# Five pairs of rounds instead of four convolved by VectorE, in a short convolution fused with a multiplicative feed-forward

## The chip, the cores and the metric

One core of a Trainium2 chip. The metric is the device time of one execution in microseconds (us); a time given for a kernel is the median of several runs. The engines are TensorE (PE in the profile; its weight loads are PEld), VectorE (DVE), ScalarE (ACT), GpSimd (POOL) and SyncE (SP). Each runs its own instructions in order; they wait for each other through semaphores. SP issues most DMAs (queue SPq) and computes nothing; GpSimd issues the DMAs that convert float32 to bfloat16 on the way (queue POOLq).

## The reference

`x` is 8 sequences of 3904 tokens with 192 channels. Each of 8 heads (24 channels each) has 7 taps, normalised by a softmax; every channel is convolved along its sequence, causally, with its head's taps. The result, 31232 x 192, goes through a feed-forward with a product in the middle:

```
w = exp(weight - max); w = w / (sum(w) + 1e-09)        # (8, 7)
out[b, s, h*24+g] = sum_k w[h, k] * x_padded[b, s + k, h*24+g]
a = x @ w1 ; b = x @ w2                                # 192 -> 1024
h = (a * b) @ w3 ;  return h @ w_out                   # 1024 -> 1024 -> 192
```

Weights are float32 at the interface; the kernel computes in bfloat16 with float32 accumulation.

## The kernel before

`w3` and `w_out` are multiplied once at the start into `W_sb` (1024 x 192), so that each token needs two products: the first, `x @ w1` and `x @ w2` with the product of both, and the second, that times `W_sb`.

The tokens are seen as two streams of TS = 15616 tokens (`NS` = 2, four sequences each) that go side by side: one on partitions 0 to 63, one on 64 to 127. A round R is 512 tokens of each stream; there are 31 rounds, the last of 256. The channels stand in three groups of 64 (`NP` = 3). `first_product(R)` (L471) makes for each of 8 blocks of 128 features `pa` and `pb` in PSUM (6 matmuls of 64 x 512 each), ScalarE copies `pa` to `asb` (L493), VectorE multiplies it with `pb` into `abT` (L495). `second_product(R, r)` (L505) makes 32 matmuls into `ops`, ScalarE copies them to `osb` (L516), SP sends that out (L521). PSUM has four slots of two banks, which `pa`, `pb`, `ops` and the convolution's `cps` take in turn; `osb` has five buffers.

The instructions are emitted in an order written out by hand: a start with rounds 0 to 2, in which weights are loaded and swapped between partition halves and `W_sb` is made (`w3_turn`, `w3_product`), and then phases (L672). Phase 0 has no first products; phase p from 1 to 14 has the first products of rounds 2p + 1 and 2p + 2. After them each phase has the second products of rounds 2p and 2p + 1 (the last phase: all that are left), so these run two rounds or more behind.

The convolved operand of the first products is made in one of two ways.

By TensorE: the tokens are cut into windows of 32 that give 26 results each, gathered in batches (`SIZES`, windows per stream). `x_jobs` has GpSimd's DMA queue load a batch as bfloat16 into `xb`; `conv` (L300) multiplies it by the banded matrix `Aband` (32 x 32 pieces) into `cps`, and ScalarE (`A`) or VectorE (`V`) evicts that to `convo`; `store` (L334) writes it to DRAM (`rows`), and `transposes(R)` (L390) has SP read it back transposed into a ring of four rounds, `xT`. Batches 0 to 3 belong to the start. From batch 4 on a batch is convolved in units of 2 or 4 heads (L646), put between second products by `places` (L649). A unit of 4 heads is 64 matmuls, of 2 heads 32, which hold twice the windows each. In the phases that have a task (below) both evictions are ScalarE's, otherwise one is VectorE's (L662).

By VectorE, for the rounds of the phases in `SIDE` (4, 7, 10 and 13): one task is one channel group of one such phase, 1024 tokens of both streams. `side_cast` has GpSimd's queue copy `x` as bfloat16 to DRAM (`rows_c`, L417), one issue a stream; `side_transpose` has SP read it transposed into `raw` (L427, two issues); `side_conv` (L430) multiplies by the second-last tap into the float32 sum `acc` (L437), adds five products (L444) and writes the seventh tap's sum to `side`. Where a sequence begins inside the task, the five sums are made in two pieces. The taps come from `wC`, which SP loads (L403) and GpSimd copies to the second partition half (L674). A task runs in one of the three phases ahead of its own, so phases 1 to 12 have one task each. `side_conv` is emitted ahead of the second products. `operand` (L454) reads `side` or `xT`.

GpSimd's DMA jobs of a phase (`jobs`, L653) are spread over its first products: at `points`, GpSimd copies a corner of `abT` (`pace`, L679) and then issues a share. In the start, `later_loads` (L614) issues the loads of batch 3, of `w_out` and `w3`, then batch 4, the first task's two casts, and batch 5.

Of the kernel before, what the change touches and what calls it, by code (L numbers as in the profile page):

```python
# [8 lines left out]
FP32 = mybir.dt.float32  # L9
BF16 = mybir.dt.bfloat16  # L10
AX = mybir.AxisListType
ALU = mybir.AluOpType
ACT = mybir.ActivationFunctionType
# [3 lines left out]
def kernel(  # L17
# [10 lines left out]
    nc = tc.nc  # L28

    B, S, D = x.shape  # L30
    H, K = weight.shape
    G = D // H
# [4 lines left out]
    NS = 2  # L37
    TS = B * S // NS
    CH = 512
    NR = -(-TS // CH)  # L40
    RING = 4 * CH
    LAG = 2
    Q = 64
    NP = D // Q
    C = 32
    ST = C - PAD
    LAG_ROWS = (LAG + 1) * CH
    SIDE = (4, 7, 10, 13)
    SIZES = [20, 20, 20, 40, 40, 40, 80, 80, 80, 32]
    NB = len(SIZES)  # L50
    FIRST = [sum(SIZES[:b]) for b in range(NB)]
    XN = 20 * D
# [2 lines left out]
    def phase_of(R):  # L55
        return (R - 1) // 2
# [10 lines left out]
    conv_rounds = [R for R in range(NR) if phase_of(R) not in SIDE]  # L67
    ring_of = {R: i for i, R in enumerate(conv_rounds)}
    t0 = (LAG + 3) * CH
    spans = [(0, t0), (t0, t0 + SIZES[4] * ST), (t0 + SIZES[4] * ST, (2 * SIDE[0] + 1) * CH)]  # L70
    for q, nxt in zip(SIDE, SIDE[1:] + (NR,)):
        spans.append(((2 * q + 3) * CH, min((2 * nxt + 1) * CH, TS)))
    wins = []
    for i, (t0, t1) in enumerate(spans):
        ws = windows(t0, t1)
        size = sum(SIZES[:4]) if i == 0 else SIZES[3 + i]
# [85 lines left out]
    def load_x(b):  # L162
        for part in range(len(parts_of(b))):
            for f in x_jobs(b, part):
                f()
# [107 lines left out]
    p = group(1, 0).start  # L273
# [130 lines left out]
                              in_=taps_d[h:h + 1, :].to_broadcast([c1 - c, K]))  # L404
            c = c1

    raw_of, side_of = {}, {}

    def side_span(p):
        return (2 * p + 1) * CH, (2 * p + 3) * CH  # L410

    def side_cast(p, k):
        t0, t1 = side_span(p)

        def job(r):
            def run():
                nc.gpsimd.dma_start(  # L417
                    out=rows_c[t0 - HALO:t1, k, r * Q:r * Q + Q],
                    in_=x_rows[r * TS + t0 - HALO:r * TS + t1, k * Q:k * Q + Q])
            return run  # L420
        return [job(r) for r in range(NS)]

    def side_transpose(p, k):
        t0, t1 = side_span(p)
        raw_of[p, k] = stage.tile([128, HALO + 2 * CH], BF16, tag="w3T", bufs=2, name="raw")
        for lo, hi in ((t0 - HALO, t0 + CH), (t0 + CH, t1)):
            nc.sync.dma_start_transpose(  # L427
                out=raw_of[p, k][:, HALO + lo - t0:HALO + hi - t0], in_=rows_c[lo:hi, k, :])

    def side_conv(p, k):  # L430
        t0, t1 = side_span(p)
        if p not in side_of:
            side_of[p] = stage.tile([128, NP, 2 * CH], BF16, tag="w3b0", bufs=1, name="side")
        raw = raw_of.pop((p, k))
        acc = stage.tile([128, 2 * CH], FP32, tag="w3b4", bufs=1, name="acc")
        starts = [z for z in range(0, TS, S) if t0 <= z < t1]
        nc.vector.tensor_scalar(  # L437
            out=acc, in0=raw[:, HALO - 1:HALO - 1 + t1 - t0], scalar1=wC[:, k, K - 2:K - 1],
            scalar2=None, op0=ALU.mult)
        for z in starts:  # L440
            nc.vector.memset(acc[:, z - t0:z - t0 + 1], 0.0)

        def add(out, lo, hi, d):
            nc.vector.scalar_tensor_tensor(  # L444
                out=out, in0=raw[:, HALO + lo - t0 - d:HALO + hi - t0 - d],
                scalar=wC[:, k, K - 1 - d:K - d], in1=acc[:, lo - t0:hi - t0],
                op0=ALU.mult, op1=ALU.add)

        for d in range(2, K):
            for lo, hi in zip([t0] + [z + d for z in starts], starts + [t1]):  # L450
                add(acc[:, lo - t0:hi - t0], lo, hi, d)
        add(side_of[p][:, k, :], t0, t1, 0)

    def operand(R, k, rs):  # L454
        if phase_of(R) in SIDE:
            t0 = R * CH - side_span(phase_of(R))[0]
            return side_of[phase_of(R)][rs, k, t0:t0 + width(R)]
        a = ring_of[R] * CH % RING
        return xT[k][rs, a:a + width(R)]
# [45 lines left out]
    def second_product(R, r):  # L505
        ab = abT_of[R]
        ng = width(R) // 128
        ops = banks("ops")
        for g in range(ng):
            for jt in range(JT):  # L510
                nc.tensor.matmul(  # L511
                    ops[:, g // 2, (g % 2) * D:(g % 2) * D + D],
                    ab[:, jt, r, g * 128:(g + 1) * 128], W_sb[:, jt, :],
                    start=(jt == 0), stop=(jt == JT - 1))
        osb = slot([128, ng, D], FP32, "osb")
        nc.scalar.copy(out=osb.rearrange("p (a g) d -> p a (g d)", g=2),  # L516
                       in_=ops[:, 0:ng // 2, 0:2 * D])
        n = ng if R < NR - 2 else ng // 2
        for g in range(0, ng, n):
            t0 = r * TS + R * CH + g * 128  # L520
            (nc.scalar if g and (R, r) == (NR - 1, NS - 2) else nc.sync).dma_start(  # L521
                out=out[t0:t0 + n * 128, :].rearrange("(g p) d -> p g d", p=128),
                in_=osb[:, g:g + n, :])
        if r == 1:
            del abT_of[R]
# [79 lines left out]
        swap_w(k, HC + 256, DFF, P)  # L605
    load_w3(0, 4, range(2, 4))

    def seq(*fs):
        def run():
            for f, *a in fs:  # L610
                f(*a)
        return run

    def later_loads():  # L614
        nc.gpsimd.tensor_scalar(out=taps, in0=taps, scalar1=total, scalar2=None, op0=ALU.mult)
        load_x(3)
        load_wo()
        load_w3(4, 2)
        load_w3(6, 2)
        load_x(4)  # L620
        for f in side_cast(SIDE[0], 0):
            f()
        load_x(5)

    first_product(0, {
        0: seq((swap_w, 1, 256, HC, A, (1,))),
# [11 lines left out]
               (conv, 3, 0, 96, (A,), (0,)), (conv, 3, 0, 96, (V,), (1,))),  # L638
        4: seq((w3_product, 4), (w3_product, 6),
               (conv, 3, 96, 96, (A,), (0,)), (conv, 3, 96, 96, (V,), (1,)),  # L640
               (store, 3), (transposes, 3), (transposes, 4))})


    phases = [()] + [(R, R + 1) for R in range(LAG + 1, NR, 2)]
    assert phases[-1][-1] == NR - 1
    units = [(b, h, n) for b in range(4, NB)  # L646
             for n in [max(v for v in (2, 4) if v * shape_of(b)[1] * G <= CH)]
             for h in range(0, H, n)]
    places = {0: (0, 1), 1: (0, 2), 2: (2,), 3: (0, 1, 2), 5: (0, 2), 6: (0, 2),  # L649
              8: (0, 2), 9: (0, 2), 10: (0,), 11: (0,)}  # L650
    assert sum(map(len, places.values())) == len(units)
    tasks = {q - NP + k: (q, k) for q in SIDE for k in range(NP)}
    jobs = {p: side_cast(*tasks[p + 1]) for p in range(1, len(phases)) if p + 1 in tasks}  # L653
    for p, b, part in ((1, 6, 0), (2, 6, 1), (3, 7, 0), (4, 7, 1), (6, 8, 0), (7, 8, 1), (9, 9, 0)):
        jobs[p] = jobs.get(p, []) + x_jobs(b, part)
    points = ((0, 1), (0, 3), (0, 5), (0, 7), (1, 2), (1, 4))
    sent = [LAG + 3]
    due = []

    def convolve(p):  # L660
        b, h, n = units.pop(0)
        conv(b, h * G, n * G, (V, A) if p not in tasks else (A, A))  # L662
        if h + n == H:
            store(b)
            while sent[0] < len(conv_rounds) and \
                    min((conv_rounds[sent[0]] + 1) * CH, TS) <= spans[b - 3][1]:
                due.append(conv_rounds[sent[0]])
                sent[0] += 1
# [1 line left out]
    pace = const.tile([1, 2], BF16)  # L670
    done = 0
    for p, rounds in enumerate(phases):  # L672
        if p == 0:
            P(out=wC[Q:128], in_=wC[0:Q])  # L674
        todo = jobs.pop(p, [])

        def issue(R, ft, n):
            def run():
                P(out=pace, in_=abT_of[R][0:1, ft, 1, 0:2])  # L679
                for _ in range(min(n, len(todo))):  # L680
                    todo.pop(0)()
            return run

        each = -(-len(todo) // len(points))
        for j, R in enumerate(rounds):
            first_product(R, {ft: issue(R, ft, each) for a, ft in points if a == j and todo})
        assert not todo
        for b in {u[0] for u in units[:3]}:
            for xb, p0, w in zero_rows.pop(b, []):
                nc.gpsimd.memset(xb[p0:p0 + PAD, w, :], 0.0)  # L690
        if p + 1 in tasks:
            side_transpose(*tasks[p + 1])
        if p in tasks:
            side_conv(*tasks[p])
        last = NR if p == len(phases) - 1 else done + 2
        seconds = [(R, r) for R in range(done, last) for r in range(NS)]
        done = last
        for n, (R, r) in enumerate(seconds):
            (last_product if (R, r) == (NR - 1, NS - 1) else second_product)(R, r)
            if n in places.get(p, ()):  # L700
                convolve(p)
        for R in due[:2]:
            transposes(R)
        del due[:2]
# [31 lines left out]
```

## Time and profile before

| what | us |
|---|---|
| median of 3 runs | 516.99 (516.53 to 517.62) |
| profiled execution, its own time | 516.74 |
| its span | 514.9 |
| second products of phase 0 begin | 52.25 |
| first products of phase 1 begin | 64.44 |
| first products of phase 14 begin | 482.47 |
| last matmuls begin | 510.17 |

The span is what lies between the first and the last instruction; 1.84 us of the run lie around it. The profile's groups give the busy time of all instructions of one line and shape, their mean in ns, and after the bar the idle time of that engine just before them with what ended it. In the chain of waits, time is put down to the work that the end waited for. A row of the stretch view has the busy time of each engine between two times, a bracket behind each with the instructions. A matmul's end is modelled, so a busy TensorE is not by itself a TensorE at its peak. The granted TensorE clock of the profiled execution is 0.999.

### The profile page before, as it was taken

How to read it: one execution, taken by the hardware profiler on the slowest of the kernel's cores; microseconds unless marked ns; L12 is line 12 of the kernel's file. 1: busy time of each engine (PE TensorE's matmuls, PEld its weight loads, DVE VectorE, ACT ScalarE, POOL GpSimd, SP SyncE). 2: the span in 40 equal slices, each digit the busy share in tenths (PEclk: the TensorE clock that was granted, in tenths of full speed). 3: DMA queues.
4: the chain of work that ended last, by engine and by line, in shares of the span. 5: the costliest groups of instructions: out<-in, count | busy, mean ns of one | idle time of the engine just before them, and what ended most of it. 6: DMA issues, size and time to landing. Idle time of an engine off the chain costs nothing.

```text
span 514.9 us, 14364 instructions
## 1 busy us (share of the span) xinstructions
PE 510.1 (99%) x6148; PEld 334.5 (65%) x6148; DVE 418.2 (81%) x410; ACT 340.2 (66%) x392; POOL 90.3 (18%) x191
## 2 busy tenths in 40 slices
PE   9999999999999999999999999999999999999997
PEld 4446946758567585675856758567585675846787
DVE  7898389699796997979979899797997979977370
ACT  7786476674768737677576475767747657376562
POOL 9965021040220401002030010320101000000000
PEclk9999999999999999999999999999999999999999
DMA  9999599898575998039599872835949171210304
GB/s 141 150 166 185 123 163 203 166 146 153 71 96 138 184 153 160 23 124 82 105 150 179 187 72 80 106 45 144 155 115 144 23 190 27 75 51 1 123 1 155
DMA packets 149744, 61.19 MB, mean 119 GB/s; under 512 B 102708, under 2 KB 149680, under 8 KB 149680
## 3 DMA queue, kind: packets, MB, share of 16 engines
q1 hardware_dynamic: 88848, 42.73, 37.3%
q0 software_dynamic: 60672, 17.44, 35.0%
q8 instruction: 48, 0.79, 0.6%
q14 instruction: 16, 0.13, 0.1%
q10 hardware_dynamic: 160, 0.10, 0.1%
HBM read 35.16 MB, written 34.85 MB: 136 GB/s over the span
## 4 chain that ended last, share of the span: by engine, by line
PE 95%; POOL 3%; ACT 0%; issue 0%; DVE 0%; POOLq 0%
PE ops L511 32%; PE pa L486 30%; PE pb L486 30%; PE cps L318 2%; POOL ws L214 1%; PE wps L579 1%; POOL xb L152 1%; PE tps L365 0%; PE ops L532 0%; DVE abT L495 0%; POOL w3b L560 0%; POOL wn L220 0%; POOL wn L221 0%; POOL wn L223 0%; POOL wn L222 0%
## 5 line engine op out<-in xcount | busy, mean ns | idle before, releaser
L495 DVE TENSOR_TENSOR abT<-asb,pb 128x1024 bf16<-128x1024 bf16 x240 | 292.9, 1221 | 71.6 <-ACT asb L493 56.0
L493 ACT CAST asb<-pa 128x1024 bf16<-128x1024 f32 x244 | 247.0, 1012 | 63.3 <-PE pa L486 63.1
L486 PEld LDWEIGHTS <-wn 64*128 64x128 bf16 x1488 | 138.2, 94 | 85.1 <-issue 2.2
L486 PEld LDWEIGHTS <-ws 64*128 64x128 bf16 x1488 | 131.1, 94 | 71.3 <-POOL ws L214 1.1
L511 PE MATMUL ops<-W_sb,abT 128*128 128x192 bf16 x1936 | 165.5, 247 | 0.0
L511 PEld LDWEIGHTS <-abT 128*128 128x128 bf16 x1936 | 158.1, 98 | 8.5 <-issue 8.1
L486 PE MATMUL pb<-xT,wn 64*128 64x512 bf16 (+1 forms) x552 | 146.7, 372 | 0.0
L486 PE MATMUL pa<-xT,wn 64*128 64x512 bf16 (+1 forms) x552 | 145.8, 372 | 0.2
L486 PE MATMUL pa<-xT,ws 64*128 64x512 bf16 (+1 forms) x552 | 145.9, 372 | 0.0
L486 PE MATMUL pb<-xT,ws 64*128 64x512 bf16 (+1 forms) x552 | 144.7, 372 | 0.1
L516 ACT COPY osb<-ops 128x768 f32<-128x768 f32 (+1 forms) x61 | 48.4, 793 | 99.0 <-PE ops L511 99.0
L444 DVE SCALAR_TENSOR_TENSOR acc<-raw,wC,acc 128x1024 f32<-128x1024 bf16 (+10 forms) x90 | 78.7, 925 | 1.3
L679 POOL COPY pace<-abT 1x2 bf16<-1x2 bf16 x52 | 9.1, 174 | 282.7 <-DVE abT L495 282.7
L486 PE MATMUL pb<-side,wn 64*128 64x512 bf16 x192 | 52.0, 376 | 0.0
L486 PE MATMUL pa<-side,wn 64*128 64x512 bf16 x192 | 51.8, 376 | 0.0
L486 PE MATMUL pa<-side,ws 64*128 64x512 bf16 x192 | 51.8, 377 | 0.0
L486 PE MATMUL pb<-side,ws 64*128 64x512 bf16 x192 | 51.4, 376 | 0.0
L152 POOL DMA_DIRECT2D xb<-in_x_dram x64 | 40.8, 642 | 13.0 <-issue 6.3
L327 ACT CAST convo<-cps 128x640 bf16<-128x640 f32 (+4 forms) x70 | 39.1, 637 | 1.6 <-PE cps L318 1.5
L417 POOL DMA_DIRECT2D rows_c<-in_x_dram x24 | 18.6, 778 | 6.9 <-issue 6.9
L444 DVE SCALAR_TENSOR_TENSOR side<-raw,wC,acc 128x1024 bf16<-128x1024 bf16 x12 | 15.4, 1285 | 0.4
L318 PE MATMUL cps<-xb,Aband 32*32 32x120 bf16 (+2 forms) x1088 | 13.3, 233 | 0.0
(65 smaller groups left out, 101.4 us busy)
## 6 DMA issues: line engine op xcount, KB each, us to landing
out_dram<-osb SPq DMA_DIRECT2D x58, 384.0 KB
xb<-in_x_dram POOLq DMA_DIRECT2D x28, 240.0 KB, 6.4
rows_c<-in_x_dram POOLq DMA_DIRECT2D x24, 130.0 KB, 4.8
rows<-convo SPq DMA_DIRECT2D x9, 240.0 KB
xb<-in_x_dram POOLq DMA_DIRECT2D x8, 228.0 KB, 10.4
rows<-convo SPq DMA_DIRECT2D x9, 150.0 KB
xb<-in_x_dram POOLq DMA_DIRECT2D x8, 168.0 KB, 4.4
rows<-convo SPq DMA_DIRECT2D x9, 120.0 KB
```

Of the source, the lines that this page charges most:

```text
L152: nc.gpsimd.dma_start(out=tiles[js[0]][0][group(r, e), s:s + w, :], in_=bass.AP(tensor=x.tensor, offset=(r * TS + t - PAD) * D, ap=[[D, C] ...
L214: f(out=wsw[k][Q * h:Q * h + Q, lo:hi], in_=wn[k][Q - Q * h:2 * Q - Q * h, lo:hi])
L318: nc.tensor.matmul(o.rearrange("p (w g) -> p w g", g=wd)[:, :, c - c0:c1 - c0], Aband[group(r, e), h, :], xb[group(r, e), s:s + m, c:c1], ...
L327: f(out=convo[:, e::E, k, :, lo:lo + c] .rearrange("p w r g -> p r w g"), in_=src[:, :, :, o:o + c])
L417: nc.gpsimd.dma_start(out=rows_c[t0 - HALO:t1, k, r * Q:r * Q + Q], in_=x_rows[r * TS + t0 - HALO:r * TS + t1, k * Q:k * Q + Q])
L444: nc.vector.scalar_tensor_tensor(out=out, in0=raw[:, HALO + lo - t0 - d:HALO + hi - t0 - d], scalar=wC[:, k, K - 1 - d:K - d], in1=acc[:, ...
L486: nc.tensor.matmul(p[:, r, f * N:f * N + N], w_of(i, k, r)[rs, ft * 128:(ft + 1) * 128], operand(R, k, rs), start=(k == 0), stop=(k == NP ...
L493: nc.scalar.copy(out=asb[:, :, 0:per * N], in_=pa[:, :, 0:per * N])
L495: nc.vector.tensor_tensor(out=ab[:, f0, :, 0:N], in0=asb[:, :, 0:N], in1=pb[:, :, 0:N], op=ALU.mult)
L511: nc.tensor.matmul(ops[:, g // 2, (g % 2) * D:(g % 2) * D + D], ab[:, jt, r, g * 128:(g + 1) * 128], W_sb[:, jt, :], start=(jt == 0), stop ...
L516: nc.scalar.copy(out=osb.rearrange("p (a g) d -> p a (g d)", g=2), in_=ops[:, 0:ng // 2, 0:2 * D])
L679: P(out=pace, in_=abT_of[R][0:1, ft, 1, 0:2])
```

## The change

`SIDE` becomes (3, 6, 9, 12, 14): five phases, the last with 768 tokens a stream instead of 1024 (rounds 29 and 30). The batches become 20, 20, 20, 40, 40, 80, 80, 80, 40: one batch less than before, 420 windows instead of 452, in 16 units from batch 4 on instead of 18. `spans` is worked out in a loop and begins a new batch after each `SIDE` phase.

The fifteen tasks (five phases by three groups) are laid out one after the other over the phases from 0 on, by a room of 6.8 sums a phase where a sum of 1024 tokens counts 1 and of 768 counts 0.75. This gives one task each in phases 0 to 11, in phase 12 one and a half of the shorter tasks and in phase 13 the other one and a half. A task's first product, by the second-last tap, is made by ScalarE (`side_first`), and VectorE makes six sums (`side_sums`). `side_steps`, called ahead of each second product, emits them: the first product at its place n, the sums as soon as their task's first product has been emitted. For the tasks of phases 0 to 12 that begin a phase, n is 0.

There are now two `acc`, five `raw` and two `side` buffers, taken once in `side_tiles`, in space that `w3b` and `w3T` had in the start, and one `side` of its own. Task 0's casts are issued in `later_loads` ahead of batch 4, and task 1's behind it, followed by the first half of batch 5; the other casts go to the phases' `jobs`, ahead of what they have or behind it where there are fewer than six. Task 0's transposes are emitted in R2's first products, ahead of the store of batch 3 and the transposes of rounds 3 and 4; the copy of `wC` to the second half moves from GpSimd in phase 0 to ScalarE just before them. The other tasks' transposes stay one phase ahead, ahead of the second products.

The output copies of rounds 26 (second stream) to 28 are sent in two halves, as those of rounds 29 and 30 were.

```diff
-    SIDE = (4, 7, 10, 13)
-    SIZES = [20, 20, 20, 40, 40, 40, 80, 80, 80, 32]
+    SIDE = (3, 6, 9, 12, 14)
+    SIZES = [20, 20, 20, 40, 40, 80, 80, 80, 40]
...
     def side_span(p):
-        return (2 * p + 1) * CH, (2 * p + 3) * CH
+        return (2 * p + 1) * CH, min((2 * p + 3) * CH, TS)
+
+    tasks = [(q, k) for q in SIDE for k in range(NP)]
+    side_of, acc_of, raw_of = {}, [], []
+    RAW = HALO + 2 * CH
+
+    def side_tiles():
+        for _ in range(2):
+            t = stage.tile([128, 2 * RAW], BF16, tag="w3T", bufs=2, name="raw")
+            raw_of.extend((t[:, 0:RAW], t[:, RAW:2 * RAW]))
+        for tag in ("w3b4", "w3b6"):
+            acc_of.append(stage.tile([128, 2 * CH], FP32, tag=tag, bufs=1, name="acc"))
+        a = stage.tile([128, NP * 2 * CH + RAW], BF16, tag="w3b0", bufs=1, name="side")
+        raw_of.append(a[:, NP * 2 * CH:])
+        b = const.tile([128, NP * 2 * CH], BF16, name="side")
...
-    def side_conv(p, k):
+    def side_first(i):
+        p, k = tasks[i]
         t0, t1 = side_span(p)
...
-        nc.vector.tensor_scalar(
-            out=acc, in0=raw[:, HALO - 1:HALO - 1 + t1 - t0], scalar1=wC[:, k, K - 2:K - 1],
-            scalar2=None, op0=ALU.mult)
+        nc.scalar.activation(
+            out=acc_of[i % 2][:, 0:t1 - t0], in_=raw_of[i % 5][:, HALO - 1:HALO - 1 + t1 - t0],
+            func=ACT.Copy, scale=wC[:, k, K - 2:K - 1])
+
+    def side_sums(i):
...
+                for lo, hi in [(t0, t1)] if last else \
+                        zip([t0] + [z + d for z in starts], starts + [t1]):
+                    a = acc[:, lo - t0:hi - t0]
+                    nc.vector.scalar_tensor_tensor(
+                        out=side_of[p][:, k, 0:t1 - t0] if last else a,
+                        in0=raw[:, HALO + lo - t0 - d:HALO + hi - t0 - d],
+                        scalar=wC[:, k, K - 1 - d:K - d], in1=a, op0=ALU.mult, op1=ALU.add)
...
+        size = (t1 - t0) / (2 * CH)
+        return [(size, job(d, d == 0)) for d in list(range(2, K)) + [0]]
...
-        n = ng if R < NR - 2 else ng // 2
+        n = ng if (R, r) < (NR - 5, 1) else ng // 2
...
+    places = {0: (0, 1), 1: (2,), 2: (0, 1, 2), 4: (0, 2), 5: (0, 2), 7: (0, 2), 8: (0, 2),
+              10: (0,), 11: (0,)}
+    starts, chain, room, p = {}, {}, 0, -1
+    for i, (q, k) in enumerate(tasks):
+        for cost, f in side_sums(i):
+            while room < cost:
+                p += 1
+                room = 6.8
...
         load_wo()
         load_w3(4, 2)
         load_w3(6, 2)
+        for i in starts[0]:
+            for f in side_cast(i):
+                f()
         load_x(4)
-        for f in side_cast(SIDE[0], 0):
+        for i in starts[1]:
+            for f in side_cast(i):
+                f()
+        for f in x_jobs(5, 0):
             f()
-        load_x(5)
...
         4: seq((w3_product, 4), (w3_product, 6),
                (conv, 3, 96, 96, (A,), (0,)), (conv, 3, 96, 96, (V,), (1,)),
+               (A, wC[Q:128], wC[0:Q]), (side_tiles,), *[(side_transpose, i) for i in starts[0]],
                (store, 3), (transposes, 3), (transposes, 4))})
...
-    places = {0: (0, 1), 1: (0, 2), 2: (2,), 3: (0, 1, 2), 5: (0, 2), 6: (0, 2),
-              8: (0, 2), 9: (0, 2), 10: (0,), 11: (0,)}
...
-        conv(b, h * G, n * G, (V, A) if p not in tasks else (A, A))
+        conv(b, h * G, n * G, (V, A) if p not in chain else (A, A))
...
-        if p == 0:
-            P(out=wC[Q:128], in_=wC[0:Q])
...
-        if p + 1 in tasks:
-            side_transpose(*tasks[p + 1])
-        if p in tasks:
-            side_conv(*tasks[p])
+        for i in starts.get(p + 1, ()):
+            side_transpose(i)
+        state = set()
...
         for n, (R, r) in enumerate(seconds):
+            side_steps(p, n, state)
             (last_product if (R, r) == (NR - 1, NS - 1) else second_product)(R, r)
             if n in places.get(p, ()):
                 convolve(p)
```

## Prediction before the result

> **What bounds the kernel now.** I read first the page's busy times and its chain of waits, then the stretches by phase. A phase is the stretch from one first product of a round pair to the next; its bounds come from the chain of waits in order of time, which shows each place where TensorE goes from `ops` back to `pa`.
>
> ```profile
> PE 510.1 (99%) x6148; PEld 334.5 (65%) x6148; DVE 418.2 (81%) x410; ACT 340.2 (66%) x392; POOL 90.3 (18%) x191
> PE 95%; POOL 3%; ACT 0%; issue 0%; DVE 0%; POOLq 0%
> ```
>
> TensorE is busy for 99% of the span and makes 95% of the chain; no wait of it for another engine has a share worth naming. Busy alone would not settle it, so I looked at what a phase costs with and without a given piece of work:
>
> ```profile
> 64.44:97.46 33.02, 33.02 (x451) 21.68 (x452) 27.92 (x23) 23.05 (x28) 5.35 (x12) 1.00 1.12 187
> 129.42:162.29 32.87, 32.87 (x418) 21.20 (x420) 27.91 (x23) 24.77 (x30) 5.36 (x12) 1.00 0.61 96
> 162.29:193.79 31.50, 31.50 (x323) 20.73 (x324) 28.19 (x29) 19.35 (x20) 6.04 (x12) 1.00 1.15 163
> 354.95:387.24 32.29, 32.29 (x387) 21.19 (x388) 27.92 (x23) 20.89 (x24) 2.26 (x6) 1.00 0.69 136
> 387.24:419.48 32.24, 32.24 (x387) 21.29 (x388) 27.92 (x23) 20.88 (x24) 2.22 (x6) 1.00 0.55 100
> 419.48:450.98 31.50, 31.50 (x323) 20.71 (x324) 27.92 (x23) 19.35 (x20) 0.00 (x0) 1.00 0.27 81
> 450.98:482.47 31.49, 31.49 (x322) 20.68 (x324) 19.54 (x16) 19.34 (x20) 0.00 (x0) 1.00 0.15 51
> ```
>
> Columns: bounds, length, then the busy time of TensorE, of its weight loads, of VectorE, ScalarE and GpSimd, the granted clock, the DMA share, GB/s. These are phases 1, 3, 4, 10, 11, 12 and 13. Phases 4, 12 and 13 have no TensorE convolution: all take 31.5 us. That phase 13 has no VectorE task (19.54 us busy against 27.92) and takes the same time shows that VectorE's work is hidden. Phases 4 and 13 read their rounds from `side`, phase 12 from `xT`: the operand's place costs nothing. Phase 1 has two convolution units of 4 heads and takes 1.52 us more; phases 10 and 11 have one each, 0.79 and 0.74 more; phase 3 has three units of 2 heads, 1.37 more. So a unit costs TensorE's time, 0.74 to 0.79 or 0.46 us, and nothing that VectorE does shows.
>
> **What it removes and adds on TensorE.** 128 matmuls go, and with them two units. Before, the 4-head units are those of batches 4 (phase 0), 5 (phase 1) and 9 (phases 10 and 11): six. After, they are those of batches 4 (phase 0) and 8 (phases 10 and 11): four. The 2-head units are twelve both times (batches 6, 7, 8 become 5, 6, 7). Priced by the phases: gone 1.52 (phase 1) + 0.79 + 0.74 (phases 10, 11) = 3.05; new in phases 10 and 11, two 5-window units at phase 1's price, 1.52. Net **-1.53 us**. First and second products keep their number; rounds that change their operand's place cost 0, by phases 4, 12 and 13.
>
> **What VectorE and ScalarE get.**
>
> ```profile
> L444 DVE SCALAR_TENSOR_TENSOR acc<-raw,wC,acc 128x1024 f32<-128x1024 bf16 x30 | 38.5, 1285 | 1.1
> L444 DVE SCALAR_TENSOR_TENSOR acc<-raw,wC,acc 128x128 f32<-128x128 bf16 x15 | 5.2, 346 | 0.1
> L437 DVE TENSOR_SCALAR acc<-raw,wC 128x1024 f32<-128x1024 bf16 x12 | 9.0, 748 | 0.0
> 84.67 1.01 ACT L493 CAST asb<-pa 128x1024 bf16<-128x1024 f32 x1 [0.28 <-PE pa L486]
> 88.05 0.80 ACT L516 COPY osb<-ops 128x768 f32<-128x768 f32 x1 [2.38 <-PE ops L511]
> 484.31 2.52 DVE L495 TENSOR_TENSOR abT<-asb,pb 128x1024 bf16<-128x1024 bf16 x2 [10.85 <-ACT asb L493]
> ```
>
> A task is now six sums on VectorE, 6 x 1.285 = 7.7 us, instead of 0.75 + 7.7; a task that crosses a batch start has eleven pieces, about 8.9 us (by the line between 346 ns at 128 and 1285 at 1024, 1.05 ns a column). Tasks sit in phases 0 to 11 one each; phases 12 and 13 hold nine shorter sums each (768 columns: 1017 ns by that line). The second products give 10.7 us of TensorE without need of VectorE, and its last `abT` ends 1.7 us into them (phase 13: second products begin at 471.74, VectorE's idle time before 484.31 is 10.85, so it stopped at 473.46). Phases 0 to 12 end their tasks by 1.7 + 8.9 = 10.6 us at most, before VectorE's next `abT` at about 12.5. Cost 0. Phase 13 is the narrow one: 473.46 + 9 x 1.032 (with the 15 ns between two sums) = 482.75, and the third pair of R29's first matmuls reads what the last sum writes, at 482.85 in the trace of before. Bounds: 0, or, if each sum is priced as a full one, 2.3 us late; nearer is the 1017. I take **+0.05**.
>
> ScalarE gets one product a task. Its shape has no row; the nearest are the cast of 128x1024, 1.01 us, and below it the 128x1 ACTIVATE of this kernel, 0.20. I take 1.0. It falls into the 2.38 us in which ScalarE waits for the first `ops` of each phase, so 0; without that cover it would hold up the `osb` copy, which frees the PSUM slot that TensorE takes again two blocks later. From below, VectorE's 0.75 us less a task gains nothing, as phase 13 showed. In phase 0 the unit's evictions go from V and A to A alone, as phase 1's were: the 1.53 us that phase 0 takes above 10.66 equal phase 1's 1.52, so 0. The copy of `wC` (0.20 us on GpSimd) is now behind the fifth `asb` of R2 on ScalarE, when that engine runs without a gap: `asb`, `abT` and the slot they free come 0.2 later; at most +0.2, **+0.05** taken, because the next `asb` already waited 0.28 us for TensorE.
>
> **The start, where queues are passed.**
>
> ```profile
> 34.17 6.77 SPq L403 DMA_DIRECT2D wC<-taps_d  x10
> 49.63 4.64 SPq L356 DMA_DIRECT2D rows<-convo  x8
> 54.90 9.68 SPq L390 DMA_TRANSPOSE xT<-rows  x6
> 64.69 2.50 SPq L427 DMA_TRANSPOSE raw<-rows_c  x2
> 48.40 0.20 POOL L674 COPY wC<-wC 64x21 f32<-64x21 f32 x1
> ```
>
> Task 0's two transposes are put on SP ahead of batch 3's stores. They wait for task 0's two casts and for the third `w3` product to let go of its `w3T` buffer, both inside SP's idle stretch from 40.9 to 49.6: that product runs in 44.85 to 47.59, so the transposes issue between 46.2 and 50.1 (1.25 us each, as the 2.50 for two shows). On GpSimd the casts now come before batch 4's loads, which passes batch 4 by two issues of 0.79 us; batch 4's unit is run at 55.0, its loads landed at 45.7 by the landing records. Two more casts and eight fewer, larger `x` issues by four: the software queue, full until 52.7, stays so about 1.8 us longer (two casts landed 0.9 us apart each). Behind SP's new transposes wait the stores, and behind these the transposes of R3 and R4. R3's last landed at 61.1 and is read at 64.44: 3.3 us of slack. Pushed by 0.5 us of issue and 1.8 of DMA, it still lands by 63.4. Cost 0 from this row; the far end, if the queue serves the new transposes as slowly as the 8 us from issue to landing that casts took there, is raw landing at 56, ScalarE's queue held from 52.7 to 57 and about 1 us lost. I take 0, since transposes issued at 87.3 and 88.6 beside other traffic landed 4.5 to 5.4 us later.
>
> The store and load DMAs of one batch fewer, and the out copies of rounds 26 to 28 split in two (0.37 us more of SP each, SP being idle 2.3 us of every 2.6 there), cost 0.
>
> **Sum.** 516.74 (the profiled execution; span 514.9 and 1.84 around it) - 1.53 + 0.05 + 0.05 = 515.2. The median shown is 516.99, 0.25 above the profiled run, so **515.5**, 0.3% less.
>
> **The rivals.**
>
> *VectorE is the bound after all* (3%). The Trainium skill's "Perfetto Trace Analysis" (Identifying the Most-Contended Engine) calls matmul busy time a poor measure and would have weight loads and the other engines' occupancy looked at, which here are 65% and 81%. What follows, from rows: VectorE's tasks grow from 103.5 us to about 115 (9 x 7.8 + 3 x 8.9 + 3 x 6.1) less 2.4 of phase 0's evictions, 9 us in all, and the time would be 526. Phase 13 against phase 12 speaks against it.
>
> *The start* (slower; 9%). SP and ScalarE run in order; if task 0's `raw` lands late, ScalarE's first product holds `osb` and both evictions of phase 0, and the R3 transposes come late too. It decides from a landing at about 56 on, each us then costing one; with landing at 60 and R3 at 67 TensorE loses 4: 519.5. For it: the DMA share is at its highest in 42 to 52. Against: 3 us of slack on each side.
>
> *Given back* (25%). The 1.5 us is small, and phase 13's 0.1 us of margin plus a start late by under 1 us can take 0.5 to 1.5 of it: 516.0 to 517.0, take 516.5.
>
> *The edit doesn't do what it says.* 128 fewer matmuls stand in the program, so 0.
>
> **Chances.** Forecast 63%, given back 25%, start 9%, VectorE 3%. About 0.2% (1.03 us) is what a measurement of this kernel can tell from no change. Faster by over that: 63% (to 515.96). Same: 25%. Slower: 12%. Range 514.5 to 517.6: below by the runs' scatter (0.5 under their median) and a further 0.5, above through the given-back case; the start and VectorE are left out.
>
> **What would show it.** Right: phases without a unit still 31.5, phases 10 and 11 about 32.26, the first `acc` product 1.0 us in ScalarE's gap, second products of phase 0 still starting near 52.25. Wrong: a gap of TensorE ahead of `pa` at phase 1 or 14, a no-unit phase over 31.6, an `osb` that waits for ScalarE, a product over 2.4 us.

## Result, and the profile after

| | median us | runs | ratio to before, 95% interval |
|---|---|---|---|
| before | 516.97 | 516.53 to 518.19 (11) | |
| changed | 516.05 | 514.98 to 516.80 (11) | 0.9978 [0.9970, 0.9987] |

The change gains 0.22%, or 1.1 us by the ratio (0.92 us by the medians), where 0.3%, or 1.5 us, was forecast. The profiled execution of the changed kernel took 516.05 us, its span 514.4.

The page of the changed kernel, busy times and chain of waits; its line numbers are its own (`asb` is now L519, `osb` L542, the tasks' sums L472, ScalarE's first product L454):

```profile
PE 508.5 (99%) x6020; PEld 333.9 (65%) x6020; DVE 423.7 (82%) x394; ACT 354.0 (69%) x404; POOL 90.7 (18%) x188
PE 94%; DMA 2%; ACT 2%; DVE 1%; issue 0%; SPq 0%; ACTq 0%
```

The 128 matmuls are gone, and VectorE's busy time grew by 5.5 us. New are 2% of DMA and 2% of ScalarE in the chain. The stretch view says where they are. First phase 0 of before, then the changed kernel's phases 0, 1, 10, 12 and 13 (bounds, length, busy TensorE, weight loads, VectorE, ScalarE, GpSimd, clock, DMA share, GB/s). The bounds are the matmuls' own starts here, 0.06 us ahead of those of the chain of waits:

```profile
52.19:64.38 12.19, 12.19 (x259) 11.52 (x258) 4.09 (x6) 4.81 (x8) 0.00 (x0) 1.00 0.55 116
```

```profile
52.43:65.78 13.35, 12.44 (x258) 11.66 (x256) 9.35 (x14) 7.29 (x13) 0.00 (x0) 1.00 0.73 144
65.78:97.73 31.95, 31.95 (x353) 20.79 (x352) 27.72 (x29) 22.12 (x23) 6.04 (x12) 1.00 1.08 171
387.02:419.28 32.26, 32.26 (x385) 21.47 (x384) 28.09 (x23) 23.09 (x26) 0.00 (x0) 1.00 0.26 60
419.28:450.77 31.49, 31.49 (x321) 20.61 (x320) 28.22 (x25) 20.19 (x21) 0.00 (x0) 1.00 0.39 105
450.77:482.26 31.49, 31.49 (x321) 20.65 (x320) 27.82 (x25) 20.19 (x21) 0.00 (x0) 1.00 0.16 51
```

From phase 1 on all is as forecast: 31.5 us without a unit, 31.95 with one of two heads, 32.26 in phases 10 and 11; phases 1 to 13 take 416.49 us instead of 418.03. Phase 13, now with VectorE busy for 27.82 us instead of 19.54, takes the same time. But phase 0 takes 13.35 us instead of 12.19, with TensorE idle for 0.91 of it. ScalarE's and SP's order of time in it (start, time, what; in brackets the idle time ahead and what ended it):

```profile
51.68 1.01 ACT L519 CAST asb<-pa 128x1024 bf16<-128x1024 f32 x1 [0.28 <-PE pa L512]
56.68 1.15 ACT L454 ACTIVATE acc<-raw,wC 128x1024 f32<-128x1024 bf16 x1 [3.99 <-DMA raw<-rows_c]
57.74 0.78 ACT L542 COPY osb<-ops 128x768 f32<-128x768 f32 x1
58.41 1.94 ACT L332 CAST convo<-cps 128x640 bf16<-128x640 f32 x4
```

```profile
46.34 3.09 SPq L448 DMA_TRANSPOSE raw<-rows_c  x2
49.66 7.22 SPq L361 DMA_DIRECT2D rows<-convo  x8
```

```profile
59.49 0.70 PE L323 MATMUL cps<-xb,Aband 32*32 32x120 bf16 x62 [0.69 <-ACT convo L332]
60.41 5.44 PE L537 MATMUL ops<-W_sb,abT 128*128 128x192 bf16 x64 [0.22 <-ACT convo L332]
```

The two transposes of task 0 are issued at 46.34 and 47.62, and the second has landed at 56.6, 9 us later (by the landing records, fifteen of its sixteen parts by 55.3, the last at 56.6). ScalarE's product, first in line in phase 0, waits 3.99 us for it. Behind it stand the copy of `ops`, which was ready at 55.2 and is made at 57.74, and the evictions of both units. So no PSUM slot is free for TensorE, which waits 0.69 and 0.22 us at the second unit.

SP is held by the same landing. Of the view of SP's waits (us in total, times, the longest):

```profile
SPq L361 <- DMA raw<-rows_c: 3.2, 2, 2.7
```

Two of batch 3's nine stores wait for task 0's transposes: the seventh is issued at 53.60, when the first has landed (53.59), the eighth at 56.59, when the second has (56.58). They neither read nor write what the transposes write; but in the records SP's DMAs count on eight semaphores in turn, and each of the two stores waits for the count of the transpose that had its semaphore before. That this is the reason is read from the records; no run here takes it away. R3's transposes stand behind the stores and begin at 58.30 instead of 54.90. In this kernel they still land in time: the third channel group at 63.79, for matmuls at 66.23.

The profiled executions add up: 0.21 us in the block of R2 ahead of phase 0, 1.16 in phase 0, -1.54 in phases 1 to 13, -0.46 at the end (from the last second products' start to the last instruction 16.38 us instead of 16.84), and 0.03 at the very start: -0.60, which is 514.95 to 514.35.

### The profile page after: what moved, and what is told of

Read it like the earlier page. It is cut to its first block, busy times and chain, and to the rows that moved or that the text cites. A ratio compares the mean times of both kernels' runs of the same rounds, so it can differ in the third digit from the quotient of the medians.

```text
span 514.4 us, 14105 instructions
## 1 busy us (share of the span) xinstructions
PE 508.5 (99%) x6020; PEld 333.9 (65%) x6020; DVE 423.7 (82%) x394; ACT 354.0 (69%) x404; POOL 90.7 (18%) x188
## 4 chain that ended last, share of the span: by engine, by line
PE 94%; DMA 2%; ACT 2%; DVE 1%; issue 0%; SPq 0%; ACTq 0%
PE ops L537 31%; PE pa L512 30%; PE pb L512 30%; DMA raw<-rows_c 2%; PE cps L323 2%; PE wps L605 1%; ACT convo L332 1%; PE warm L233 1%; ACT asb L519 1%; DVE abT L521 0%; PE ops L558 0%; PE tps L385 0%; SPq L448 0%; ACT acc L454 0%; PE tps L370 0%
## 5 line engine op out<-in xcount | busy, mean ns | idle before, releaser
L519 ACT CAST asb<-pa 128x1024 bf16<-128x1024 f32 x244 | 247.1, 1013 | 63.1 <-PE pa L512 62.9
L512 PE MATMUL pb<-xT,wn 64*128 64x512 bf16 x504 | 136.9, 376 | 0.0
L512 PE MATMUL pa<-xT,wn 64*128 64x512 bf16 x504 | 136.0, 376 | 0.2
L512 PE MATMUL pa<-xT,ws 64*128 64x512 bf16 x504 | 136.1, 376 | 0.0
L512 PE MATMUL pb<-xT,ws 64*128 64x512 bf16 x504 | 134.9, 376 | 0.1
L542 ACT COPY osb<-ops 128x768 f32<-128x768 f32 (+1 forms) x61 | 48.5, 795 | 81.2 <-PE ops L537 77.5
L472 DVE SCALAR_TENSOR_TENSOR acc<-raw,wC,acc 128x1024 f32<-128x1024 bf16 (+2 forms) x75 | 75.2, 1032 | 1.2
L512 PE MATMUL pb<-side,wn 64*128 64x512 bf16 (+1 forms) x240 | 61.8, 365 | 0.0
L512 PE MATMUL pa<-side,ws 64*128 64x512 bf16 (+1 forms) x240 | 61.5, 366 | 0.0
L512 PE MATMUL pa<-side,wn 64*128 64x512 bf16 (+1 forms) x240 | 61.4, 366 | 0.0
L512 PE MATMUL pb<-side,ws 64*128 64x512 bf16 (+1 forms) x240 | 61.1, 365 | 0.0
L332 ACT CAST convo<-cps 128x640 bf16<-128x640 f32 (+2 forms) x66 | 37.7, 652 | 1.6 <-PE cps L323 1.6
L472 DVE SCALAR_TENSOR_TENSOR acc<-side,wC,acc 128x1024 f32<-128x1024 bf16 (+1 forms) x15 | 17.9, 1195 | 0.4
L454 ACT ACTIVATE acc<-raw,wC 128x1024 f32<-128x1024 bf16 (+1 forms) x12 | 13.4, 1116 | 4.0 <-DMA raw<-rows_c 4.0
```

The costliest lines, as they stand in the source:

```text
L332: f(out=convo[:, e::E, k, :, lo:lo + c] .rearrange("p w r g -> p r w g"), in_=src[:, :, :, o:o + c])
L454: nc.scalar.activation(out=acc_of[i % 2][:, 0:t1 - t0], in_=raw_of[i % 5][:, HALO - 1:HALO - 1 + t1 - t0], func=ACT.Copy, scale=wC[:, k, K ...
L472: nc.vector.scalar_tensor_tensor(out=side_of[p][:, k, 0:t1 - t0] if last else a, in0=raw[:, HALO + lo - t0 - d:HALO + hi - t0 - d], scalar ...
L512: nc.tensor.matmul(p[:, r, f * N:f * N + N], w_of(i, k, r)[rs, ft * 128:(ft + 1) * 128], operand(R, k, rs), start=(k == 0), stop=(k == NP ...
L519: nc.scalar.copy(out=asb[:, :, 0:per * N], in_=pa[:, :, 0:per * N])
```

## The experiments

Theory S: the start takes back what the units gave. Task 0's transposes land late since they share the DMA engines with GpSimd's queue, still full of batch loads, and in-order ScalarE passes the delay on. Theory W: the copy of `wC` on ScalarE costs its 0.21 us. Theory T: the halved output copies shorten the end. Each kernel is an edit of the changed one.

All of them in one table. "Ahead" is the time from the last `wps` matmul to the first `ops` matmul, "product" the start of task 0's first product, in e2 and f4 on VectorE (its `raw` has then landed), "end" from the last second products' start; these columns are from the profiled execution of each, worked out from its order of time.

| kernel | median us | ratio, 95% interval | ahead | product | phase 0 | phase 1 | end |
|---|---|---|---|---|---|---|---|
| before | 516.97 | | 4.84 | | 12.19 | 33.02 | 16.84 |
| changed | 516.05 | 0.9978 [0.9970, 0.9987] | 5.05 | 56.7 | 13.35 | 31.95 | 16.38 |
| e1_wc_pool | 516.16 | 0.9984 [0.9972, 0.9995] | 4.84 | 56.6 | 13.51 | 31.95 | 16.37 |
| e2_v_first | 515.25 | 0.9968 [0.9956, 0.9980] | 5.05 | 55.7 | 12.19 | 32.18 | 16.35 |
| e3_x5_later | 521.20 | 1.0088 [1.0071, 1.0105] | 5.05 | 52.9 | 12.19 | 37.67 | 16.37 |
| e4_whole_out | 516.01 | 0.9985 [0.9974, 0.9995] | 5.05 | 55.6 | 12.19 | 31.95 | 16.67 |
| f1_x5_early1 | 521.43 | 1.0082 [1.0070, 1.0095] | 5.05 | 52.5 | 12.19 | 37.28 | 16.37 |
| f2_x5_wc | 522.01 | 1.0095 [1.0082, 1.0108] | 4.84 | 53.0 | 12.19 | 37.70 | 16.37 |
| f3_more_start | 518.25 | 1.0033 [1.0015, 1.0051] | 5.05 | 57.0 | 15.31 | 32.23 | 16.36 |
| f4_v_first_wc | 515.01 | 0.9963 [0.9950, 0.9975] | 4.84 | 56.8 | 12.19 | 32.62 | 16.37 |
| g1_x5_phase0 | 514.79 | 0.9959 [0.9946, 0.9971] | 4.84 | 53.1 | 12.19 | 31.95 | 16.37 |
| g2_whole_out | 515.14 | 0.9969 [0.9958, 0.9981] | 4.84 | 52.6 | 12.19 | 31.95 | 16.67 |
| g3_first_n1 | 515.65 | 0.9976 [0.9967, 0.9985] | 5.05 | 58.2 | 12.19 | 33.93 | 16.38 |

Phases 2 to 13 take 384.5 us in every one of them, to 0.03, against 385.0 before.

**The copy of wC**

```diff
-               (A, wC[Q:128], wC[0:Q]), (side_tiles,), *[(side_transpose, i) for i in starts[0]],
+               (P, wC[Q:128], wC[0:Q]), (side_tiles,), *[(side_transpose, i) for i in starts[0]],
```

> The changed kernel with the copy of wC to the second partition half back on GpSimd (same place in the order). Theory W (a copy of 0.21 us on ScalarE, in a stretch where it has no gap, is passed on to TensorE): the 0.4 us that TensorE waits for a PSUM slot in R2's last block goes, second products of phase 0 begin at 52.2 instead of 52.43; phase 0 itself stays near 13.4 us, because the late raw is untouched. Time 0.2 us less than the changed kernel's 516.05, so 515.85. Rival (the 0.24 us come from the start of the run, not from the copy): second products still begin at 52.4.

The stretch ahead of phase 0 falls from 5.05 to 4.84 us, the value of before: theory W holds, to the length of the copy. The time did not fall (516.16 and 516.05, with runs that scatter over 2.6 and 1.8 us), as phase 0 in this profile is 13.51. What e1 saves ahead is waited for in phase 0, whose end hangs on the landing.

**Task 0's first product on VectorE**

```diff
     def side_first(i):
...
+        if i == 0:
+            nc.vector.tensor_scalar(out=out, in0=in_, scalar1=wC[:, k, K - 2:K - 1],
+                                    scalar2=None, op0=ALU.mult)
+            return
         nc.scalar.activation(out=out, in_=in_, func=ACT.Copy, scale=wC[:, k, K - 2:K - 1])
```

> Only task 0's first product goes back to VectorE; ScalarE then waits for nothing in phase 0 that comes from a DMA. Theory S (task 0's raw lands at 56.6, and the first product that waits for it holds ScalarE's output copies and evictions, queued behind it): ScalarE's 4.0 us of waiting go, the 0.69 and 0.22 us that TensorE waits for evictions go, phase 0 takes about 12.2 us instead of 13.4; raw still lands near 56.6; VectorE's task ends near 66 and may cost phase 1 a few tenths. Time 515.0 to 515.2. Rival A (both evictions on ScalarE and its product, 1.15 us, are simply too much for phase 0): phase 0 stays at 13 us or more less the 1.15 of the product, no matter that ScalarE no longer waits.

515.25 us, and the runs lie within 0.8 us (514.83 to 515.65) instead of 1.8. Phase 0 is back at 12.19 with ScalarE doing both units' evictions. Rival A is not ended by that, since 13.35 less the product's 1.15 is 12.2 too; it falls with e3, e4 and g1 below, where ScalarE has the evictions and the product, `raw` lands earlier, and phase 0 takes 12.19. For theory S, too, this profile proves less than it seems: its `raw` had landed by 55.4, and e4 shows that 55.45 does no harm even with the product on ScalarE. f4 settles it.

> e2 (task 0's first product on VectorE) and the copy of wC on GpSimd. The late landing stays, ScalarE does not wait for it. Theory W adds 0.2 us to e2's gain: 515.0. What stays is the 0.2 us of R3's late transposes at the start of phase 1 that e2's profile shows (32.18 against 31.95). Rival (e2's gain was a good landing in its profile and not the order): phase 0 of 13 us or more where raw lands past 56.

In f4 the landing was as late as in the changed kernel (by the landing records the last part of `raw` came at 56.56; VectorE's product begins at 56.78, and its row names a store that counts on one of the same semaphores), and yet phase 0 takes 12.19. Of the trace of f4, VectorE's product and ScalarE's order:

```profile
56.78 0.75 DVE L456 TENSOR_SCALAR acc<-raw,wC 128x1024 f32<-128x1024 bf16 x1 [2.91 <-DMA rows<-convo]
```

```profile
54.99 0.80 ACT L545 COPY osb<-ops 128x768 f32<-128x768 f32 x1 [2.38 <-PE ops L540]
55.69 1.95 ACT L332 CAST convo<-cps 128x640 bf16<-128x640 f32 x4
```

The copy of `ops` is made at 54.99, ahead of the landing: nothing waits behind it. So the loss in phase 0 was what stood behind a waiting instruction on ScalarE, not the late data as such. What f4 has left is 0.67 us in phase 1 (32.62), and it hits the first matmuls that read R3's third channel group from `xT`:

```profile
64.56 0.38 PE L515 MATMUL pa<-xT,wn 64*128 64x512 bf16 x1
65.43 0.37 PE L515 MATMUL pa<-xT,wn 64*128 64x512 bf16 x1 [0.49 <-DMA xT<-rows]
```

R3's transposes are late too, and by the same landing, for SP is held as in the changed kernel:

```profile
SPq L361 <- DMA raw<-rows_c: 4.1, 2, 2.8
```

The eighth store is issued at 56.58, 0.02 us after `raw` has landed; then SP waits 1.6 us for the stores to land, R3's transposes begin at 59.06, and the third group has landed at 65.39, for matmuls that could have begun at about 64.8.

**One place later on ScalarE**

```diff
-                chain.setdefault(p, []).append((i, n, lambda i=i: side_first(i)))
+                chain.setdefault(p, []).append((i, 1 if i == 0 else n, lambda i=i: side_first(i)))
```

> The changed kernel with task 0's first product one place later in ScalarE's order: behind the first output copy and the first unit's evictions of phase 0. Nothing else moves; raw still lands at 55 to 57. Theory S (what is lost in phase 0 is what stands behind the waiting product): phase 0 takes 12.2 us though raw is late; VectorE ends its task near 68 and may cost phase 1 up to 1 us; time 515.2 to 515.6. Rival (the loss comes from TensorE's own operands, R3's late transposes): the time of the changed kernel, 516.05, with the loss now at the start of phase 1.

Phase 0 is 12.19 as theory S has it, with the product at 58.2. The price came elsewhere than expected: in the profiled execution (517.3, the longest of its ten) TensorE waits 1.80 us for R3's `xT`, and phase 1 takes 33.93. The median, 515.65, lies between the changed kernel and e2. So the rival is right beside S: with phase 0 mended, R3's late transposes show. They begin at 60.20, behind stores that SP held until `raw` had landed at 57.50; of the third group's sixteen parts fifteen had landed by 65.84, the last at 67.40.

**Batch 5's first half out of the start**

```diff
-        for f in x_jobs(5, 0):
-            f()
...
-    for p, b, part in ((1, 5, 1), (2, 6, 0), (3, 6, 1), (5, 7, 0), (6, 7, 1), (8, 8, 0)):
+    for p, b, part in ((1, 5, 0), (1, 5, 1), (2, 6, 0), (3, 6, 1), (5, 7, 0), (6, 7, 1), (8, 8, 0)):
```

> Only the loads of the first half of batch 5 (four issues) move from the start to the jobs of phase 1, so that GpSimd's DMA queue runs dry some 5 us earlier. Theory S with its cause (task 0's transposes, issued at 46.3 to 49.4, share the DMA engines with a queue full to 57): raw lands at 50 to 53 instead of 56.6, ScalarE's wait in phase 0 falls from 4.0 us to under 1, phase 0 takes 12.2 to 12.4 us, time 514.9 to 515.1. Rival C (a transpose that reads what a cast has just written to DRAM takes 7 to 9 us by itself, whatever else runs): raw still lands at 55 to 57, time as the changed kernel's. Rival for the loads: batch 5 is now late for its unit in phase 1, which would show as a wait of TensorE ahead of cps near 95.

The cause of the late landing is shown: with four loads fewer in the start, `raw` has landed at 52.0 instead of 56.6, and phase 0 takes 12.19. Rival C falls. The rival for the loads came true as well: in phase 1 the unit waits for batch 5, and the kernel is slower than before. Not all of the 5.7 us that phase 1 is longer is waiting. The second product behind the unit takes 4.15 us in e3, where 32 matmuls of that shape took 2.81 at the start of the changed kernel's phase 0:

```profile
98.50 4.15 PE L537 MATMUL ops<-W_sb,abT 128*128 128x192 bf16 x32
```

The granted clock is 0.50 from 97.89 to 101.30 in e3, and for 3.41 us at about the same place in f1 and f2; in the rest of phase 1 it is 1.0. So some 4.4 us are the late loads and 1.3 the clock.

f1 issues the twelve loads of phase 1 four at a time (`each = 4 if p == 1`), f2 adds the copy of `wC` on GpSimd.

> As e3 (batch 5's first half out of the start), but phase 1 issues its twelve loads four at a time at its first three points instead of two at six, so that batch 5 lands in time. Theory S: raw lands near 52.9 as in e3, phase 0 takes 12.2 us and phase 1 31.95 (in e3 37.67, for the late batch); the runs scatter less, since the loss of 0 to 1.3 us in phase 0 that depends on the landing is gone; time 514.9 to 515.2. Rival (the queue's load only moves, and the twelve issues now disturb phase 1): phase 1 over 32.2 us, and no gain over the changed kernel's 516.05.

> f1 and the copy of wC on GpSimd. In the profile of e1 the stretch from the last w3 product's last matmul to the second products fell from 5.05 to 4.84 us, what it was before the change. Theory W: the two add up, time 0.2 us under f1, 514.7 to 515.0, and the kernel is the fastest. Rival: the 0.2 us are hidden by something else that ends later; time as f1's.

Both missed: phase 1 took 37.3 and 37.7 us. The chain of waits of f1 in phase 1:

```profile
70.79 7.53 DMA xb<-in_x_dram
78.31 0.28 issue
78.59 18.32 DMA xb<-in_x_dram
96.91 0.04 issue
96.96 0.55 PE cps L323 x18
```

A load of a single window, issued at 78.6, lands at 96.9, 18 us later, behind all that was queued before it; loads of this size (12 KB) took 7.4 us in the median in the kernel before. GpSimd's queue moved 370 to 380 KB per 2 us when alone (42 to 46 us of the changed kernel) and 145 to 216 beside SP's stores and output copies (80 to 92 us of f1). Issuing earlier does not help where the queue itself is the limit. In f2 too the stretch ahead is 4.84, but its 0.2 us are lost in the scatter of the late loads.

**More into the start**

```diff
-        for f in x_jobs(5, 0):
+        for f in x_jobs(5, 0) + x_jobs(5, 1):
             f()
...
-    for p, b, part in ((1, 5, 1), (2, 6, 0), (3, 6, 1), (5, 7, 0), (6, 7, 1), (8, 8, 0)):
+    for p, b, part in ((2, 6, 0), (3, 6, 1), (5, 7, 0), (6, 7, 1), (8, 8, 0)):
```

> The opposite of f1: the second half of batch 5 (six more issues) is put into the start too, so GpSimd's queue is full some 5 to 8 us longer. Theory S, by dose: raw lands at 58 to 61, ScalarE waits 6 to 8 us in phase 0 and TensorE loses 3 to 5 us, partly behind the transposes of R3, which come later too; time 518 to 521. Rival C (the landing does not depend on the queue's load; a transpose takes its time): raw at 56 to 57 and the time within 0.3 us of the changed kernel's. Rival H (the transposes get a fixed share and are done before the added loads are reached): as C.

518.25, from 516.72 to 521.68: the dose raises the loss, at the low end of what was expected, but not by the way that I gave. `raw` landed at 56.9, hardly later than in the changed kernel; that fits rival H for the transposes (they take a share of the engines and are done before the added loads matter). What grew is the other landing. SP and TensorE in f3:

```profile
49.80 7.43 SPq L361 DMA_DIRECT2D rows<-convo  x8
59.78 8.26 SPq L395 DMA_TRANSPOSE xT<-rows  x6
```

```profile
67.87 0.37 PE L512 MATMUL pa<-xT,wn 64*128 64x512 bf16 x1 [1.67 <-DMA xT<-rows]
```

The transposes of R3 and R4 begin at 59.78 (58.30 in the changed kernel, 54.90 before), since SP waits for `raw` and then longer for the stores. The first takes 8.0 us to land, 2.5 in the changed kernel, with GpSimd's queue busy to 67.3. TensorE waits 1.67 us for R3, which the table counts in phase 0, as that lasts until the next `pa`.

**Batch 5's first half between the two**

```diff
+        if p == 0:
+            P(out=pace, in_=convo_of[4][0:1, 0, 2, 0, 0:2])
+            for f in x_jobs(5, 0):
+                f()
```

This stands at the end of phase 0, with the loads out of the start and the copy of `wC` on GpSimd.

> The four loads of batch 5's first half are issued neither in the start nor in phase 1, but at the end of phase 0, held by a copy on GpSimd until the second unit's evictions are done (about 62 us); the copy of wC is on GpSimd. Theory S: task 0's raw lands near 52.7 and R3's transposes by 61 to 62, as in e3; phase 0 takes 12.2 us and phase 1 31.95, and the stretch ahead of phase 0 4.84: span 512.9, time 514.5 to 514.8, the fastest kernel. Rival (the loads at 62 slow R4's transposes or task 1's, or make batch 5 late): phase 1 over 32.2 us, or a wait of TensorE ahead of cps near 94.

514.79 us, all five runs within 0.27: faster than both kernels, 2.1 us or 0.41% under before. GpSimd, SP and ScalarE in its trace:

```profile
60.29 0.89 POOL L772 COPY pace<-convo 1x2 bf16<-1x2 bf16 x1 [14.69 <-ACT convo L332]
61.13 2.71 POOL L157 DMA_DIRECT2D xb<-in_x_dram  x4
```

```profile
49.70 4.89 SPq L361 DMA_DIRECT2D rows<-convo  x8
54.63 0.53 SPq L354 DMA_DIRECT2D rows<-convo  x1
55.48 9.66 SPq L395 DMA_TRANSPOSE xT<-rows  x6
```

```profile
53.09 1.15 ACT L454 ACTIVATE acc<-raw,wC 128x1024 f32<-128x1024 bf16 x1 [0.36 <-DMA raw<-rows_c]
55.11 0.80 ACT L542 COPY osb<-ops 128x768 f32<-128x768 f32 x1 [0.87 <-PE ops L537]
```

The stores are issued in 4.9 us instead of 7.2, since `raw` has landed (52.9) before SP comes to those that wait for it (the view of SP's waits has no wait for `raw`); R3's transposes begin at 55.5, ScalarE's product fits into the gap that was meant for it, and its phases 0 and 1 take 12.19 and 31.95 us.

**The halved output copies**

```diff
-        n = ng if (R, r) < (NR - 5, 1) else ng // 2
+        n = ng if R < NR - 2 else ng // 2
```

> Only the output copies of rounds 26 to 28 are sent whole again. The profile of the changed kernel ends 16.42 us after the last second products begin, that of before 16.79. Theory T (the halves shorten the end): the end is 0.3 to 0.4 us longer and the time 0.3 us more than the changed kernel's. Rival (the end scatters from run to run): no difference beyond 0.2 us in the time, the end between 16.3 and 16.9.

> g1 with the output copies of rounds 26 to 28 whole again. The profiles so far end 16.35 to 16.38 us after the last second products begin with halves (seven), 16.84 and 16.67 with whole copies (two). Theory T: the end is 0.3 to 0.45 us longer, time 0.3 us over g1. Rival: no difference in the time beyond 0.15 us.

e4 against the changed kernel says nothing in time (516.01 and 516.05), since phase 0 scatters by more than what is sought; its profiled execution happened to have the landing at 55.45 and lost nothing in phase 0. On the quiet kernel it shows: g2 takes 515.14 and g1 514.79, 0.35 us, and their ends 16.67 and 16.37 us. Theory T holds. Why the end is shorter, and which of the five copies does it, was not tried; the further 0.16 us between the ends of g2 (16.67) and before (16.84) stays open.

## Why the prediction was right, and where not

- **What bounds the kernel.** Right. Tasks in phase 13 changed nothing, and phases 2 to 13 are alike to 0.03 us in the twelve kernels with the new plan. The Trainium skill's "Perfetto Trace Analysis" (Identifying the Most-Contended Engine) judges TensorE by the share of its peak rate that a kernel reaches, which was not worked out here, and by weight loads. These stayed at 65%, under VectorE's 82%, while only TensorE's work set the phases; so the measurement decides against going by weight loads alone. The rival that VectorE is the bound would have given 526.
- **The units, -1.53 us.** Right: -1.54.
- **VectorE in phase 13, +0.05.** Measured 0. The tasks lie otherwise than I laid them out: phase 11 has room for one sum of task 12 (0.8 left, 0.75 needed), so phase 13 has eight sums and ends them at 481.5, 1.2 us ahead of the matmuls that read them (482.7 at the earliest). A sum of 768 columns took 1.02 us, as interpolated.
- **ScalarE's first product, 1.0 us.** 1.15 us. The Trainium skill's "ScalarE: Activation LUTs" (What ACT_TABLE_LOAD costs) gives about 280 ns + 0.833 ns an element for an ACTIVATE with one pointer operand, by which 1.13 us would be an estimate here; the trace agrees. In the later phases it hides in ScalarE's gaps, as said: in phase 1 the wait ahead of the `osb` copy is 1.33 us instead of 2.38.
- **The copy of wC, +0.05.** Mis-sized: 0.21, the whole copy. I had the bound of 0.2 and took a quarter of it because the next `asb` waits 0.28 us for TensorE; but by the order of time the same block's `abT` begins at 50.40 instead of 50.10, and the matmuls that take its PSUM slot, R2's last `pb`, wait, before that slack comes.
- **The start, 0.** The step that failed. I chose the landing of 4.5 to 5.4 us, seen at 87 us in the trace, over the 8 us that the casts took in the very stretch into which the transposes were put, and so the cover of 2.38 us seemed enough. Measured: 9 us, landing at 56.6; the far end that I worked out (56, 1 us lost) is what happened. The change's own two additional casts make that stretch longer, which I had counted for R3's transposes but not for these; and the 1.8 us that I had GpSimd's queue stay full for longer were about 5 (the last packets of the start moved at 57.8 instead of 52.4). For R3 the working had 0.5 us of issue and 1.8 of DMA; it did not have SP's wait for `raw`, and the transposes began 3.4 us later. One of the signs that I named for being wrong came: the `osb` copy that is ready at 55.2 waits for ScalarE until 57.74.
- **The end, 0.** Mis-sized the other way: -0.46, of which the halved copies are 0.3.
- **The sum.** Its terms add up to 515.31; the 515.2 of the text is a slip. The missed terms, +0.16 + 1.16 - 0.46 - 0.05, bring it to 516.12, and the profiled execution took 516.05. That the time came within 0.6 us of the forecast is luck in part: the end, put at nothing, gave back 0.46 of what the start took. The measured 516.05 is the case I called "given back", with phase 0 as its place. The start as a case slower than before did not come, for task 0's landing is no later than 57.5 in any of the profiles; in f3 R3's came late instead.
- **Open in part:** the loss hangs on a narrow threshold. The rival "the start" had it at a landing of about 56, which fits, and each us beyond at one us, which does not: with the landing at 55.45 nothing was lost (e4), at 56.4 to 56.6 it was 1.2 to 1.3 us (e1 and the changed kernel). The changed kernel's runs spread over 1.8 us, g1's over 0.27, which fits; but the runs of before spread over 1.7 without this cause, and the landing of a timed run is not on record.

## What to carry to other kernels

Work taken off the engine that sets the end pays to the hundredth, but look at the one place where a steady plan is filled for the first time: there the transfers have the least lead and the queues are fullest. An instruction that waits for a DMA belongs, on an in-order engine, behind the work that frees other engines' buffers, or on an engine on which nothing urgent follows. The engine that issues the DMAs is such an engine too: look for what it waits for, as SP here for `raw`. Price a transfer by a row from the stretch into which it is put, and when moving loads out of a busy stretch, find one in which nothing else that is due soon needs the DMA engines: left in the start the four loads cost 1.2 us, in phase 1 over 5 (1.3 of them by the halved clock), between the two nothing.

## What the runs showed of the hardware that was not expected

Task 0's two transposes (128 x 528 and 128 x 512, from DRAM) landed 3.0 to 6.1 us after their issue where GpSimd's queue ran dry by 49 to 52 us (e3, f1, f2, g1, g2) and 7.0 to 9.2 us after it where that queue went on to 57 or more (the others); with most loads queued (f3) it was 7.3 and 9.2, hardly more than the 7.2 and 9.0 of the changed kernel. GpSimd's loads beside SP's traffic took up to 20.7 us (f1). The Trainium skill's "DMA: Bandwidth & Descriptors" (Queues, rings and completion order) says that each DMA engine goes round between the queues that have work, a packet at a time; a share that does not shrink with the length of the other queue, as in f3, fits that, though no run here shows the order of the packets.

TensorE's granted clock fell to 0.50 for 3.41 us in e3, f1 and f2, where TensorE had all but stood still for 2.8 to 3.8 us at the unit of phase 1; the waits of 1.67 us in f3 and 1.80 us in g3 left it at 1.0. Where between the two it begins to fall, no run here shows.
